# Attention and a gated MLP on one core: two heads per step, loads of 1 KB runs that Pool reshapes two pairs ahead, remainder rows of both heads at the same partitions

## The chip, the cores and the metric

The kernel runs on one NeuronCore of a Trainium2 chip. Time is in device microseconds (us). TensorE (PE) does the matrix products, VectorE (DVE) and ScalarE (ACT) the elementwise work, GpSimd (POOL) the work between SBUF tiles, and SyncE (SP) issues nearly all DMAs from one queue in program order. Each engine works through its own list in order and waits on semaphores for the others.

## The reference

With 8 batches, 8 heads, 576 rows and 64 columns per head:

```python
scores = scale * np.matmul(q, k.transpose(0, 1, 3, 2))          # scale 1/8
thresh = np.max(scores, axis=-1, keepdims=True) - tau           # tau 0.02
attn = exp(where(scores >= thresh, scores, -1e9) - max); attn /= sum(attn) + 1e-9
x = matmul(attn, v), heads side by side: (8, 576, 512)
h = np.maximum(x @ w_in, 0.0); u, v = h[..., :512], h[..., 512:]
v_n = (v - mean(v)) / np.sqrt(var(v) + 1e-06)
v_s = np.einsum('ts,bsd->btd', w_spatial, v_n) + b_spatial[None, :, None]
out = (u * v_s) @ w_out
```

## The kernel before, in words

Two heads of one batch make a **pair**; there are 32 pairs and each has a **slot** of five **steps**, c = 0 to 4. Slot s works on pair s. 576 rows are four chunks of 128 and a remainder of 64 per head. Steps 0 to 3 take one chunk of 128 query rows of both heads; step 4 takes the 64 remainder rows of both heads, head 0 on partitions 0 to 63 and head 1 on 64 to 127.

In one step PE writes the scores of both heads into a PSUM tile `s` (two buffers): the two heads' 512 main columns with K = 64 rows each (lines 368 and 370, side by side in the array) and the 64 remainder columns of both heads through a block-diagonal tile `kd` (line 372). DVE takes the negated row maximum (`negm`, line 386), ACT the exponential (`e`, line 389), and DVE then zeroes what lies below exp(-tau) of the maximum (`p`, line 402; below called the **mask**). The mask of step c is emitted in step c + 1. SP transposes `p` by DMA (`pT`), and a slot later PE multiplies it with `v` (line 218). Step 4 does the same with a block-diagonal `qd` (lines 375, 377), lines 393, 396 and 409, and one transposed tile `pTr`.

Each step also carries **fillers** for PE: in steps 0 to 2 the transposes of the next pair's q, k and remainder (lines 176 and 191), in steps 3 and 4 the product with v of the pair before (line 218, `pv`), and from slot 5 on one piece of the MLP of a finished batch. The MLP of a batch takes four slots: `moe_v` (line 248), `moe_u` (282), `moe_s` (313) and `moe_o` (343), five pieces each, piece c in step c. Slots 5, 9, 13 ... are v slots, 6, 10 ... u slots, 7, 11 ... s slots, 8, 12 ... o slots. A filler's products go into a PSUM tile `f` (two buffers); its evacuation is emitted at the start of the next step, ahead of that step's `negm` and `e`. So in the v slots ACT takes `vrel` (line 253) behind the exponentials of the step before, DVE takes bn_stats and bn_aggr of it (`st`, `mv`, lines 255 and 257) ahead of `negm`, and POOL makes the scale and the normalised `vn` (lines 259 to 266).

The order is written out by hand: engines run the instructions as the Python emits them. q, k and v of pair s + 2 are loaded after step 3 of slot s, into two buffers (`load`, lines 97 to 124, eight DMAs on SP, q and k in runs of 256 bytes); POOL copies v to bf16 (lines 121 to 124) and the remainder blocks into `qd` and `kd` (lines 201 and 203). All of `w_spatial` and the bias is shaped on POOL ahead of the first slot (lines 143 to 161). The normalised attention output `xn` goes through a DMA transpose into `xT` (line 232), on which the v slot's first product waits.

## Time and profile before

| What | us |
|---|---|
| median of 3 runs | 706.11 (704.8 to 706.26) |
| the profiled execution: time / span | 706.51 / 704.7 |
| busy: PE, DVE, ACT, POOL | 517.9, 479.0, 299.2, 209.1 |
| mean granted PE clock | 0.912 of full speed |

The profile lists each instruction with its start and duration in us from the start of the span. A row of the waits says which engine and line waited for what: total us, times, longest. In the timeline a bracket at the end of a row is the idle time of that engine ahead of the instruction and what ended it. PE's busy time counts pipelined matmuls, so it is not PE at its peak.

### The profile page before, as it was taken

The numbers are of one execution on the slowest core, as the hardware profiler recorded it, in microseconds if no ns is written. First come the engines' busy times: TensorE is split into PE (matmuls) and PEld (weight loads), VectorE is DVE, ScalarE is ACT, GpSimd is POOL, SyncE is SP. The second block draws the span as 40 slices with busy tenths as digits, with TensorE's granted clock in tenths as the row PEclk, the third lists the DMA queues.
The fourth block names the chain that finished last, engine by engine and source line by source line (L and its number), as shares of the span: only waits on it lengthen the run. The fifth ranks groups of instructions, "written<-read, shape, count | busy, mean of one in ns | idle before, by whom it ended". The sixth has DMA issues, their size and how long they took to land.

```text
span 704.7 us, 10528 instructions
## 1 busy us (share of the span) xinstructions
PE 517.9 (73%) x3712; PEld 265.5 (38%) x3712; DVE 479.0 (68%) x570; ACT 299.2 (42%) x506; POOL 209.1 (30%) x497
## 2 busy tenths in 40 slices
PE   2177775888856788578858888567896888588876
PEld 1034442444423444244424444234442444244432
DVE  0067776788837787487857888377864888578931
ACT  1044444364524544354443645245352554336332
POOL 5601112451214311344114511143112452145031
PEclk9977777899979999899988999899997999889999
DMA  6947877377956567468693779565575677838531
GB/s 169 145 101 134 147 134 155 54 141 141 179 125 115 114 121 172 102 121 139 127 197 62 144 139 182 122 110 116 107 176 112 113 141 140 195 64 139 97 103 67
DMA packets 297786, 90.94 MB, mean 129 GB/s; under 512 B 283718, under 2 KB 292422, under 8 KB 297606
## 3 DMA queue, kind: packets, MB, share of 16 engines
q1 hardware_dynamic: 296678, 88.71, 64.8%
q0 software_dynamic: 1056, 1.57, 1.4%
q8 instruction: 29, 0.48, 0.3%
q14 instruction: 23, 0.19, 0.1%
HBM read 33.31 MB, written 9.44 MB: 61 GB/s over the span
## 4 chain that ended last, share of the span: by engine, by line
PE 28%; DVE 22%; DMA 14%; SPq 11%; ACT 11%; issue 8%; POOL 5%; POOLq 0%; ACTq 0%; DVEq 0%
DVE negm L386 12%; PE s L368 10%; DMA qn<-in_q_dram 9%; ACT e L389 7%; DVE p L402 6%; SPq L104 5%; PE s L372 4%; DMA xT<-xn 3%; PE f L218 3%; PE f L176 3%; PE f L343 2%; PE f L282 2%; POOL vn L266 2%; SPq L406 2%; SPq L107 2%
## 5 line engine op out<-in xcount | busy, mean ns | idle before, releaser
L389 ACT ACTIVATE e<-s,negm 128x576 f32<-128x576 f32 x256 | 175.7, 738 | 284.0 <-DVE negm L386 284.0
L386 DVE TENSOR_REDUCE negm<-s 128x2 f32<-128x1152 f32 x128 | 172.8, 1350 | 114.2 <-PE s L372 113.6
L402 DVE SCALAR_TENSOR_TENSOR p<-e,ctau 128x1152 bf16<-128x1152 f32 x128 | 181.5, 1418 | 0.0
L368 PE MATMUL s<-kT,qT 64*128 64x512 f32 x256 | 163.3, 721 | 4.2 <-ACT e L389 3.8
L370 PE MATMUL s<-kT,qT 64*128 64x512 f32 x256 | 163.3, 721 | 0.0
L121 POOL CAST v<-vl 128x512 bf16<-128x512 f32 x32 | 19.8, 618 | 291.3 <-DMA vl<-in_v_dram 245.0
L372 PEld LDWEIGHTS s<-kd,qT 128*128 128x128 f32 x256 | 41.4, 203 | 133.2 <-issue 107.7
L372 PE MATMUL s<-kd,qT 128*128 128x128 f32 x256 | 67.4, 348 | 21.6 <-POOL kd L203 21.6
L248 PE MATMUL f<-w_in,xT 128*128 128x512 bf16 x160 | 48.8, 427 | 41.5 <-DMA xT<-xn 41.2
L255 DVE BATCH_NORM_STATS2 st<-vrel 128x6 f32<-128x512 f32 x40 | 27.7, 692 | 73.7 <-ACT vrel L253 73.5
L218 PE MATMUL f<-v,pT 128*128 128x65 bf16 x1280 | 51.1, 193 | 34.1 <-ACT vrel L253 12.9
L176 PE MATMUL f<-identf,qn 128*128 128x128 f32 x128 | 23.8, 317 | 59.0 <-DMA qn<-in_q_dram 52.0
L218 PEld LDWEIGHTS <-pT 128*128 128x128 bf16 x1280 | 49.6, 99 | 40.4 <-issue 34.3
L368 PEld LDWEIGHTS s<-kT,qT 64*128 64x128 f32 x256 | 42.9, 209 | 53.2 <-issue 36.9
L266 POOL TENSOR_SCALAR vn<-vrel,rs,nm 128x512 bf16<-128x512 f32 (+1 forms) x40 | 53.2, 1329 | 4.0
L253 ACT ACTIVATE vrel<-f 128x512 f32<-128x512 f32 x40 | 24.1, 602 | 46.4 <-PE f L248 43.3
L343 PE MATMUL f<-w_o,gT 128*128 128x512 bf16 (+1 forms) x160 | 41.4, 387 | 2.8 <-DVE xn L227 1.7
L370 PEld LDWEIGHTS s<-kT,qT 64*128 64x128 f32 x256 | 42.9, 209 | 0.0
L313 PE MATMUL f<-wsT,vn 128*128 128x512 bf16 x160 | 41.0, 390 | 2.3 <-POOL vn L266 1.4
L396 ACT ACTIVATE e<-s,negm 128x576 f32<-128x576 f32 x32 | 23.7, 741 | 40.6 <-DVE negm L393 40.6
L176 PEld LDWEIGHTS f<-identf,qn 128*128 128x128 f32 x128 | 15.9, 159 | 63.8 <-issue 63.8
L248 PEld LDWEIGHTS <-xT 128*128 128x128 bf16 x160 | 15.8, 108 | 59.1 <-DMA xT<-xn 45.5
(71 smaller groups left out, 633.0 us busy)
## 6 DMA issues: line engine op xcount, KB each, us to landing
qn<-in_q_dram SPq DMA_DIRECT2D x64, 128.0 KB, 2.9
kn<-in_k_dram SPq DMA_DIRECT2D x64, 128.0 KB, 2.8
vl<-in_v_dram SPq DMA_DIRECT2D x32, 256.0 KB, 3.0
out_dram<-o SPq DMA_DIRECT2D x32, 256.0 KB, 2.6
pT<-p SPq DMA_TRANSPOSE x128, 3.3
wsl<-in_moe_w_spatial_dram SPq DMA_DIRECT2D x1, 1152.0 KB, 6.1
qn<-in_q_dram SPq DMA_DIRECT2D x32, 32.0 KB, 2.5
kn<-in_k_dram SPq DMA_DIRECT2D x32, 32.0 KB, 2.4
```

The source lines that it names most:

```text
L176: nc.tensor.transpose(out=t[:, c * P:(c + 1) * P], in_=src[:, c, :], identity=identf)
L218: nc.tensor.matmul(out=t[:, c * 65:c * 65 + 65], lhsT=pts[i, c][:, blk, :], rhs=vt[:, h, vb, :], start=(ki == 0), stop=(ki == 4))
L248: nc.tensor.matmul(out=t, lhsT=xts[b][:, f, c * P:(c + 1) * P], rhs=w_in[:, f, 512:1024], start=(f == 0), stop=(f == 3))
L266: nc.gpsimd.tensor_scalar(out=vn_ring[b % 2][:n, c, :], in0=vrel[:n], scalar1=rs[:n], scalar2=nm[:n], op0=ALU.mult, op1=ALU.add)
L313: nc.tensor.matmul(out=t, lhsT=vn[:, c, f * P:(f + 1) * P], rhs=wsT[:, c, 0:512], start=(c == 0), stop=(c == 4))
L343: nc.tensor.matmul(out=t[:n], lhsT=gs[b][:, f, c * P:c * P + n], rhs=w_o[:, f, :], start=(f == 0), stop=(f == 3))
L368: nc.tensor.matmul(out=s[:, 0:512], lhsT=qT[A, cs], rhs=kT[A, :], start=True, stop=True)
L370: nc.tensor.matmul(out=s[:, 1024:1536], lhsT=qT[Bh, cs], rhs=kT[Bh, :], start=True, stop=True)
L372: nc.tensor.matmul(out=view(s, 512, [[448, 2], [1, 64]]), lhsT=qT[:, cs], rhs=kd_ring[i % 2], start=True, stop=True)
L386: nc.vector.tensor_reduce(out=nm, in_=both, axis=AX.X, op=ALU.max, negate=True)
L389: nc.scalar.activation(out=e[:, h, :], in_=both[:, h, :], func=ACT.Exp, bias=nm[:, h:h + 1])
L402: nc.vector.scalar_tensor_tensor(out=pt, in0=pe.rearrange("p h s -> p (h s)"), scalar=ctau, in1=pe.rearrange("p h s -> p (h s)"), op0=ALU. ...
```

## The change

- **Loads.** Pairs are loaded two at a time (four heads) in odd slots at step 0 for slots s + 3 and s + 4: q and k in two DMAs each, v in five, in runs of 1 KB, into one of two static sets `ql`, `kl`, `vl`. POOL reorders q (and scales it) and k of pair s + 2 at step 1 of slot s (`shape_qk`) and casts v of pair s at step 0 (`shape_v`).
- **Remainder rows.** q and k of a pair now lie in one tile `qkT` of 576 columns, with both remainders in columns 512 to 575. Step 4 is four products of 64 x 64 by 288 columns (two heads, two halves); head 0 writes partitions 0 to 63 of `s`, head 1 partitions 64 to 127 of the same columns. `qd` is gone. `kd`'s product now comes ahead of the other two. The masked remainder is transposed by two DMAs, one per head, into columns 0 to 63 and 64 to 127 of `ptr`, so that both heads' remainders lie at the same partitions; the copy at line 235 is gone.
- **w_spatial** is shaped on POOL in five parts in steps 6 to 10 counted from the start, and the bias in step 12.
- **Steps.** There are two fillers, sorted so that those that ACT evacuates come first. The first, if ACT evacuates it, is evacuated ahead of the step's exponentials, else by DVE behind `negm`; the second, if DVE evacuates it, at the end of its own step, else at the start of the next. The MLP runs 27 steps behind (25 before).
- **Normalisation.** For batches 0 to 6 ACT sums `vrel` as it writes it, POOL makes the negated mean `nmean`, and ACT takes a Square with that bias and a sum in the place of bn_stats and bn_aggr; POOL makes the scale and `vn`. The last batch keeps bn_stats and has `vn`, the u evacuations and every second output copy on DVE.

Where rows move. The order of POOL's instructions at the start, before (`wsb` is the shaped `w_spatial`, the `br` rows are the bias; the block tiles come last):

```order
L143 CAST wsb<-wsl 64x512
L146 CAST wsb<-wsl 64x64
L155 CAST bhi<-brow 1x576
L156 TENSOR_TENSOR br_210<-brow,bhi 1x576
L157 CAST bmid<-br_210 1x576
L158 TENSOR_TENSOR br_211<-br_210,bmid 1x576
L159 CAST blo<-br_211 1x576
L201 TENSOR_SCALAR qd_118<-rem 64x64
L203 COPY kd_116<-rem 64x64
```

and now, from the last fill on:

```order
L94 MEMSET vn_112 64x512
L146 TENSOR_SCALAR qn<-ql_113 128x640
L149 COPY kn<-kl_114 128x640
L229 COPY kd_127<-qkT 64x64
L230 COPY kd_127<-qkT 64x64
L146 TENSOR_SCALAR qn<-ql_113 128x640
L149 COPY kn<-kl_114 128x640
L155 CAST v_107<-vl_115 128x10x64
L146 TENSOR_SCALAR qn<-ql_116 128x640
```

The block tile `kd` of pair 0, on which the first step's scores wait, stood behind all of `wsb` and the bias and now stands behind pair 0's q and k alone; the fills of the new tiles come ahead of it.

SP's queue around the first v slot, before (`qn` to `vl` are the loads of pair 6; the row of `xT` is batch 0's last):

```order
L406 DMA_TRANSPOSE pT<-p_105 128x9x128
L104 DMA qn<-in_q_dram 128x4x64 x2
L107 DMA qn<-in_q_dram 64x2x64
L104 DMA kn<-in_k_dram 128x4x64 x2
L107 DMA kn<-in_k_dram 64x2x64
L112 DMA vl<-in_v_dram 128x2x256
L115 DMA vl<-in_v_dram 64x2x64
L117 DMA vl<-in_v_dram 64x64
L406 DMA_TRANSPOSE pT<-p_106 128x9x128
L232 DMA_TRANSPOSE xT<-xn 128x5x128
L412 DMA_TRANSPOSE pTr<-pr_108 128x5x128
```

and now:

```order
L260 DMA_TRANSPOSE xT<-xn 128x5x128
L437 DMA_TRANSPOSE pT<-p_103 128x9x128
L111 DMA ql_113<-in_q_dram 128x4x256
L114 DMA ql_113<-in_q_dram 64x4x64
L111 DMA kl_114<-in_k_dram 128x4x256
L114 DMA kl_114<-in_k_dram 64x4x64
L122 DMA vl_115<-in_v_dram 128x2x256
L123 DMA vl_115<-in_v_dram 64x2x64
L125 DMA vl_115<-in_v_dram 64x2x256
L127 DMA vl_115<-in_v_dram 64x2x256
L129 DMA vl_115<-in_v_dram 64x2x64
L443 DMA_TRANSPOSE ptr_144<-pr_105 128x5x64
```

The transpose into `xT` moves from behind a group of loads to ahead of one; a group now serves two pairs.

POOL in the steps of `moe_v`, before and now (`rs` is the scale, `nm` its product with the mean):

```order
L259 TENSOR_SCALAR rs<-mv 128x1
L261 TENSOR_TENSOR rs<-rs,mhalf 128x1
L263 TENSOR_SCALAR nm<-mv,rs 128x1
L266 TENSOR_SCALAR vn_114<-vrel,rs,nm 128x512
L121 CAST v_113<-vl 128x2x4x64
```

```order
L311 TENSOR_SCALAR vn_111<-vrel,rs,nm 128x512
L155 CAST v_109<-vl_118 128x10x64
L146 TENSOR_SCALAR qn<-ql_113 128x640
L149 COPY kn<-kl_114 128x640
L299 TENSOR_SCALAR nmean<-sm 128x1
L307 TENSOR_SCALAR rs<-ss 128x1
L309 TENSOR_TENSOR rs<-rs,mhalf 128x1
L310 TENSOR_TENSOR nm<-nmean,rs 128x1
```

ACT's Square of a piece waits for `nmean`, which now stands behind the `vn` of the pieces ahead and behind three instructions of 640 columns.

The diff, cut to its core:

```diff
+    ld_ring = [[const.tile([P, 4, 5, D], F32, name=f"{n}{i}") for n in ("ql", "kl", "vl")]
+               for i in range(2)]
...
+    def load_qk(i, n):
+
+        b, hp = divmod(i, HP)
+        for t, src in zip(ld_ring[i // 2 % 2], (q, k)):
+            t = t[:, 2 * (i % 2):2 * (i % 2) + 2 * n]
+            src = src[b, 2 * hp:2 * hp + 2 * n]
+            nc.sync.dma_start(
+                out=t[:, :, 0:4, :],
+                in_=src[:, 0:512, :].rearrange("h (p c) d -> p h (c d)", c=4))
+            nc.sync.dma_start(out=t[0:64, :, 4, :],
+                              in_=src[:, 512:576, :].rearrange("h p d -> p h d"))
+
+    def load_v(i):
+        b, hp = divmod(i, HP)
+        vv = ld_ring[i // 2 % 2][2].rearrange("p (j h) c d -> p j (h c) d", h=2)
+        va = v[b, 2 * hp:2 * hp + 4].rearrange("(j h) s d -> h j s d", h=2)
+        fold = "j (p c) d -> p j (c d)"
+        nc.sync.dma_start(out=vv[:, :, 0:4, :], in_=va[0, :, 0:512, :].rearrange(fold, c=4))
+        nc.sync.dma_start(out=vv[0:64, :, 4, :],
+                          in_=va[0, :, 512:576, :].rearrange("j p d -> p j d"))
+        nc.sync.dma_start(out=vv[64:128, :, 5:9, :],
+                          in_=va[1, :, 0:256, :].rearrange(fold, c=4))
+        nc.sync.dma_start(out=vv[0:64, :, 6:10, :],
+                          in_=va[1, :, 256:512, :].rearrange(fold, c=4))
+        nc.sync.dma_start(out=vv[64:128, :, 9, :],
+                          in_=va[1, :, 512:576, :].rearrange("j p d -> p j d"))
...
+    def shape_qk(i):
...
+        for w, nm in enumerate(("qn", "kn")):
+            t = qkn.tile([P, 5, 2, D], F32, name=nm)
+            src = ld_ring[i // 2 % 2][w][:, 2 * j:2 * j + 2].rearrange("p h c d -> p c h d")
+            if w == 0:
+                nc.gpsimd.tensor_scalar(out=t, in0=src, scalar1=scale, scalar2=0.0,
+                                        op0=ALU.mult, op1=ALU.add)
+            else:
+                nc.gpsimd.tensor_copy(out=t, in_=src)
...
+    def shape_v(i):
+        j = i % 2
+        nc.gpsimd.tensor_copy(
+            out=v_ring[i % 4][:, :, 0:D],
+            in_=ld_ring[i // 2 % 2][2][:, 2 * j:2 * j + 2].rearrange("p h c d -> p (h c) d"))
...
+        nc.gpsimd.dma_start(
+            out=brow[0:1, 0:512].rearrange("o (c p) -> o c p", c=4),
...
-        for c in range(5):
-            n = P if c < 4 else 64
-            nc.gpsimd.tensor_copy(
-                out=wsb[:n, c, 0:512].rearrange("p (sc sp) -> p sc sp", sc=4),
-                in_=wsl[:n, c, 0:512].rearrange("p (sp sc) -> p sc sp", sc=4))
-            nc.gpsimd.tensor_copy(out=wsb[:n, c, 512:576], in_=wsl[:n, c, 512:576])
-        for c in range(5):
-            nc.sync.dma_start_transpose(out=wsT[:, :, c * P:(c + 1) * P], in_=wsb[:, c, :])
...
+    def shape_ws(c):
...
+        nc.sync.dma_start_transpose(out=wsT[:, :, c * P:(c + 1) * P], in_=wsb[:, c, :])
...
-            nc.scalar.activation(out=dst, in_=hold["t"], func=ACT.Copy,
...
+            nc.scalar.copy(out=qks[i][:, which, 0:512], in_=hold["t"])
...
-                nc.gpsimd.tensor_scalar(out=qd_ring[i % 2][hs, hs], in0=rem[hs, 0:64],
-                                        scalar1=scale, scalar2=0.0, op0=ALU.mult, op1=ALU.add)
-                nc.gpsimd.tensor_copy(out=kd_ring[i % 2][hs, hs], in_=rem[hs, 64:128])
...
+        def ev():
+            nc.scalar.copy(
+                out=qks[i][:, :, 512:576],
+                in_=hold["t"][:, 0:256].rearrange("p (w s) -> p w s", w=2)[:, :, 0:64])
+            kd = kd_ring[i % 2]
+            nc.gpsimd.tensor_copy(out=kd[0:64, 0:64], in_=qks[i][0:64, 1, 512:576])
+            nc.gpsimd.tensor_copy(out=kd[64:128, 64:128], in_=qks[i][64:128, 1, 0:64])
...
-                nc.gpsimd.tensor_copy(out=xts[b][64:128, hp, 512:576],
-                                      in_=xts[b][64:128, hp, 576:640])
...
-            nc.vector.bn_stats(out=st, in_=vrel)
-            mv = small.tile([P, 2], F32, name="mv")
-            nc.vector.bn_aggr(out=mv, in_=st)
...
+            if b == B - 1:
+                nc.scalar.activation(out=vrel, in_=hold["t"], func=ACT.Relu)
...
+                nc.vector.tensor_scalar(out=rs, in0=mv[:, 1:2], scalar1=1e-6, scalar2=1.0,
+                                        op0=ALU.add, op1=ALU.mult)
+                nc.gpsimd.tensor_tensor(out=rs, in0=rs, in1=mhalf, op=ALU.pow)
+                nc.vector.tensor_scalar(out=dst, in0=vrel[:n], scalar1=mv[:n, 0:1],
+                                        scalar2=rs[:n], op0=ALU.subtract, op1=ALU.mult)
...
+            nc.scalar.activation(out=vrel, in_=hold["t"], func=ACT.Relu, accum_out=sm)
+            nmean = small.tile([P, 1], F32, name="nmean")
+            nc.gpsimd.tensor_scalar(out=nmean, in0=sm, scalar1=-1.0 / 512, scalar2=0.0,
                                     op0=ALU.mult, op1=ALU.add)
...
+            def rest():
+                sq = vr.tile([P, 512], BF16, name="sq")
+                ss = small.tile([P, 1], F32, name="ss")
+                nc.scalar.activation(out=sq, in_=vrel, func=ACT.Square, bias=nmean,
+                                     accum_out=ss)
+                nc.gpsimd.tensor_scalar(out=rs, in0=ss, scalar1=1.0 / 512, scalar2=1e-6,
+                                        op0=ALU.mult, op1=ALU.add)
+                nc.gpsimd.tensor_tensor(out=rs, in0=rs, in1=mhalf, op=ALU.pow)
+                nc.gpsimd.tensor_tensor(out=nm, in0=nmean, in1=rs, op=ALU.mult)
+                nc.gpsimd.tensor_scalar(out=dst, in0=vrel[:n], scalar1=rs[:n], scalar2=nm[:n],
+                                        op0=ALU.mult, op1=ALU.add)
+            later.append(rest)
...
+            if f < 4 and b == B - 1:
+                nc.vector.tensor_scalar(out=us[b][:, f, 0:512], in0=t, scalar1=0.0, scalar2=0.0,
+                                        op0=ALU.max, op1=ALU.add)
...
+            if b == B - 1 and c % 2:
+                nc.vector.tensor_copy(out=o[:n], in_=hold["t"][:n])
...
+            return nc.tensor.matmul(out=out, lhsT=qk[hs, 0, m], rhs=qk[hs, 1, lo:lo + n],
+                                    start=True, stop=True)
+        if c < 4:
+            nc.tensor.matmul(out=view(s, 512, [[448, 2], [1, 64]]),
+                             lhsT=qk[:, 0, c * P:(c + 1) * P], rhs=kd_ring[i % 2],
+                             start=True, stop=True)
+            mm(0, s[:, 0:512], 0, 512)
+            mm(1, s[:, 1024:1536], 64, 512)
...
+        for lo, off in ((0, 224), (288, 512)):
+            for h in range(2):
+                mm(h, s[64 * h:64 * h + 64, off:off + 288], lo, 288)
...
+            dst = ptr_ring[i % 3]
+            nc.sync.dma_start_transpose(out=dst[:, :, 0:64], in_=pt[0:64, 64:704])
+            nc.sync.dma_start_transpose(out=dst[:, :, 64:128], in_=pt[64:128, 0:640])
...
+            s = scores(i, c)
+        while held:
+            held.pop(0)()
+        if f1:
+            f1[1]()
+            if f1[0] == "act":
+                f1[2]()
+        if i is not None:
+            nh = 2 if c < 4 else 1
+            nm = small.tile([P, 2], F32, name="negm")
+            nc.vector.tensor_reduce(out=nm[:, 0:nh], in_=s, axis=AX.X, op=ALU.max, negate=True)
+        if f1 and f1[0] == "dve":
+            f1[2]()
+        done = list(later)
+        later.clear()
...
+        if unmasked:
+            mask()
...
+        for f in done:
+            f()
+        if f2:
+            f2[1]()
+            if f2[0] == "dve":
+                f2[2]()
             else:
...
-        for mm, ev in fillers:
-            mm()
-            pend_ev.append(ev)
...
+                held.append(f2[2])
...
+    LAG = 27
...
+        load_qk(0, 1)
+        shape_qk(0)
+        for f in (qk_main(0, 0), qk_main(0, 1), qk_rem(0)):
+            f[1]()
+            f[2]()
+        load_qk(1, 1)
+        shape_qk(1)
+        load_v(0)
+        load_qk(2, 2)
+        load_v(2)
...
+            if i is not None:
+                if c == 1 and slot + 2 < NPAIR:
+                    shape_qk(slot + 2)
+                if c == 0:
+                    shape_v(slot)
+                if c == 0 and slot % 2 and slot + 3 < NPAIR:
+                    load_qk(slot + 3, 2)
+                    load_v(slot + 3)
+                if g == 3:
+                    load_weights()
+                if 6 <= g <= 10:
+                    shape_ws(g - 6)
+                if g == 12:
+                    shape_bias()
+            fs = []
+            if slot + 1 < NPAIR and c < 3:
+                fs.append(qk_rem(slot + 1) if c == 2 else qk_main(slot + 1, c))
+            if 1 <= slot <= NPAIR and c >= 3:
+                fs.append(pv(slot - 1, c - 3))
+            if g >= LAG:
+                fs.append(moe_job(g - LAG))
+            fs.sort(key=lambda f: f[0])
+            step(i, c, fs[0] if fs else None, fs[1] if len(fs) > 1 else None)
+        while held:
+            held.pop(0)()
```

280 lines of the change are left out of this document (107 added, 173 removed).

## The prediction

> **What bounds the kernel now.** I read the busy times first, then the waits, then the timeline of DVE from one row maximum to the next, because each step has exactly one and they mark its pace.
>
> ```profile
> PE 517.9 (73%) x3712; PEld 265.5 (38%) x3712; DVE 479.0 (68%) x570; ACT 299.2 (42%) x506; POOL 209.1 (30%) x497
> DVE negm L386 <- PE s L372: 113.6, 65, 32.3
> DVE st L255 <- ACT vrel L253: 73.5, 24, 7.9
> PE f L176 <- DMA qn<-in_q_dram: 52.0, 28, 5.0
> PE s L372 <- POOL kd L203: 21.6, 1, 21.6
> ```
>
> No engine is full: PE, the busiest, is busy 517.9 of a span of 704.7. The waits form loops, and where they lie differs by slot. These are the starts of slot 0, of slot 2 with the two row maxima after it, and of slots 5, 17, 18, 19 and 31:
>
> ```profile
> 33.19 1.36 DVE L386 TENSOR_REDUCE negm<-s 128x2 f32<-128x1152 f32 x1 [32.29 <-PE s L372]
> 64.56 1.35 DVE L386 TENSOR_REDUCE negm<-s 128x2 f32<-128x1152 f32 x1
> 70.41 1.36 DVE L386 TENSOR_REDUCE negm<-s 128x2 f32<-128x1152 f32 x1 [3.78 <-PE s L372]
> 73.01 1.35 DVE L386 TENSOR_REDUCE negm<-s 128x2 f32<-128x1152 f32 x1
> 115.48 1.35 DVE L386 TENSOR_REDUCE negm<-s 128x2 f32<-128x1152 f32 x1
> 361.75 1.36 DVE L386 TENSOR_REDUCE negm<-s 128x2 f32<-128x1152 f32 x1 [0.86 <-PE s L372]
> 390.45 1.32 DVE L386 TENSOR_REDUCE negm<-s 128x2 f32<-128x1152 f32 x1
> 406.11 1.36 DVE L386 TENSOR_REDUCE negm<-s 128x2 f32<-128x1152 f32 x1 [0.36 <-PE s L372]
> 652.51 1.36 DVE L386 TENSOR_REDUCE negm<-s 128x2 f32<-128x1152 f32 x1 [0.31 <-PE s L372]
> ```
>
> The span divides into 33.2 before the first step, 82.3 for slots 0 to 4 (115.48 - 33.19), 537.0 for slots 5 to 30 (652.51 - 115.48), and 52.2 from there to the end. A v slot took 28.7 (361.75 to 390.45), the u slot behind it 15.7 (to 406.11). Seven of the 26 slots in the middle are v slots, and they take 7 x 28.7 = 201 of the 537.
>
> In slot 2 the first step takes 5.85 (64.56 to 70.41) and the next 2.60. The 3.25 between them is the wait of PE's transposes for the q that SP has only just loaded. A v slot has two stalls:
>
> ```profile
> 277.60 1.28 SPq L104 DMA_DIRECT2D qn<-in_q_dram  x2
> 286.14 1.21 SPq L232 DMA_TRANSPOSE xT<-xn  x1
> 288.81 0.61 PE L248 MATMUL f<-w_in,xT 128*128 128x512 bf16 x1 [6.27 <-DMA xT<-xn]
> 298.34 1.37 ACT L389 ACTIVATE e<-s,negm 128x576 f32<-128x576 f32 x2 [2.35 <-DVE negm L386]
> 299.75 0.62 ACT L253 ACTIVATE vrel<-f 128x512 f32<-128x512 f32 x1
> 300.40 0.70 DVE L255 BATCH_NORM_STATS2 st<-vrel 128x6 f32<-128x512 f32 x1 [0.83 <-ACT vrel L253]
> 301.29 1.32 DVE L386 TENSOR_REDUCE negm<-s 128x2 f32<-128x1152 f32 x1
> ```
>
> First, SP issues a whole group of loads from 277.60 before the transpose into `xT` at 286.14, and PE stands 6.27 for it. Second, each of the following steps is a closed loop: exponentials 1.37, then `vrel` .62 behind them, then `st` .70, then the row maximum that the next exponentials need. ACT and DVE take turns.
>
> **The change part by part.** *Start.* The first row maximum, at 33.19, waits 21.6 for `kd`, which stands on POOL behind `wsb` and the bias. Those move to steps 6 to 12. What is left on POOL ahead of it: the fills (.15 to .5 each; they end at 5.2 before, and I put the larger set's end at 7.5), then q and k reshaped. For a reshaping of 640 columns the nearest row is
>
> ```profile
> L121 POOL CAST v<-vl 128x512 bf16<-128x512 f32 x32 | 19.8, 618 | 291.3 <-DMA vl<-in_v_dram 245.0 <-PE f L176 26.9 <-PE f L313 11.0
> L261 POOL TENSOR_TENSOR rs<-rs,mhalf 128x1 f32<-128x1 f32 x40 | 22.1, 554 | 3.3
> L143 POOL CAST wsb<-wsl 128x512 bf16<-128x512 f32 x4 | 4.3, 1070 | 0.9 <-DMA wsl<-in_moe_w_spatial_dram 0.9
> ```
>
> 618 ns x 640/512 = .77. A cast that collects single elements took 1.07 for 512, so 1.34 for 640 is the dear end; the new ones move runs of 64 elements, as L121 does, and write 4 bytes, so I take .9. Then 7.5 + .9 + .9 = 9.3, transposes of k 1.1 at the low clock, two copies .9, two `kd` copies .5 (64 columns each, so below L121's .62), cold scores 2.8: first row maximum near 14.5, **-18.7**. Later fills or dearer copies would cost up to 3.
>
> *Slots 0 to 4.* q and k are now loaded two to three slots ahead and reshaped at step 1 for use two slots on, so the 3.25 goes: 16.9 - 3.25 = 13.65 a slot, where DVE alone sets the pace. The shaping of `w_spatial` (4 x 1.07 + 1.06 and five small ones), the bias and the weights' DMA issues now lie on POOL inside these slots. I add 4 for a backlog that reaches `kd`. 5 x 13.65 + 4 = 72.3 against 82.3: **-10**, bounds -14 and 0.
>
> *Slots 5 to 30, other than v.* Here PE's own work is the floor:
>
> ```profile
> L375 PE MATMUL s<-kT,qd 128*128 128x512 f32 x64 | 33.2, 600 | 2.1 <-ACT e L389 2.1
> 73.29 0.69 PE L368 MATMUL s<-kT,qT 64*128 64x512 f32 x1
> 74.67 0.51 PE L218 MATMUL f<-v,pT 128*128 128x65 bf16 x11
> 390.41 0.63 PE L176 MATMUL f<-identf,qn 128*128 128x128 f32 x4 [1.03 <-DMA qn<-in_q_dram]
> 393.78 0.66 PE L176 MATMUL f<-identf,kn 128*128 128x128 f32 x4 [0.40 <-ACT qT L180]
> 394.27 1.03 PE L282 MATMUL f<-xT,w_in 128*128 128x512 bf16 x4
> 395.23 0.69 PE L368 MATMUL s<-kT,qT 64*128 64x512 f32 x1
> 399.85 0.80 PE L218 MATMUL f<-v,pT 128*128 128x65 bf16 x20
> ```
>
> From start to start, a chunk's scores take 1.38 (73.29 to 74.67), a set of transposes .49, an MLP piece .96, a product with v .80 (399.85). A slot is 4 x 1.38 + 2 x .49 + 5 x .96 + 2 x .80 + remainder scores 1.1 (two of .60 in line 375, that overlap) and transposes .3 = 14.3. The best whole slot, the u slot from 390.45, took 15.66 and holds the 1.03 wait for q, which goes. I take **15.1** for u and o slots (.8 of hand-overs left). In s slots DVE is the longer: two of its steps stand 3.20 apart (334.68 to 337.88), .60 over the 2.60, so 13.65 + 5 x .6 = **16.65**; nothing of that is touched.
>
> ```profile
> 334.68 1.35 DVE L386 TENSOR_REDUCE negm<-s 128x2 f32<-128x1152 f32 x1
> 337.88 1.36 DVE L386 TENSOR_REDUCE negm<-s 128x2 f32<-128x1152 f32 x1
> 298.38 1.83 POOL L266 TENSOR_SCALAR vn<-vrel,rs,nm 128x512 bf16<-128x512 f32 x1
> 151.21 0.77 POOL L266 TENSOR_SCALAR vn<-vrel,rs,nm 128x512 bf16<-128x512 f32 x1
> 151.39 1.79 DVE L402 SCALAR_TENSOR_TENSOR p<-e,ctau 128x1152 bf16<-128x1152 f32 x1
> 302.54 1.41 DVE L402 SCALAR_TENSOR_TENSOR p<-e,ctau 128x1152 bf16<-128x1152 f32 x1
> ```
>
> *SP and the small moves.* A slot's issues change by one more transpose (1.21, as at 286.14; the remainder takes two) and 3.5 fewer loads (.64 each, from 277.60), so SP loses about 1 a slot. The loads that `xT` passes land 1.2 later, and nobody wants them for two slots. The block tile's product now comes first in a step, at the same length. `qd` and the copy at line 235 leave POOL some .7 a slot, which I count against the queue's gaps. Evacuating a filler ahead of the exponentials, or on DVE behind `negm`, lets `f` come free in the same step; while PE sets the pace its evacuation (.6 to .7) has a step of 2.6 to 3.2 to hide in, so **0**; were it on the path in all 65 steps of the u and o slots, 65 x .6 = 39 and a time of 615, which the range holds.
>
> *v slots.* Three things go: the `xT` wait (its transpose now stands ahead of the loads, and the MLP runs two steps later), the q wait, and bn_stats, for which ACT does a Square (.6 like `vrel`) in its idle 58%. What is new is a chain over POOL: `vrel`'s sum, `nmean`, Square, scale, `vn`. ACT's Square stands in the next step behind that step's exponentials and waits for `nmean`; behind a late Square stand the next evacuation and exponentials, hence DVE. So the question is whether POOL keeps up. A piece costs it the power .55 (line 261), `vn` .77 (151.21) and three smaller instructions on one column, which with gaps I put at .9: 2.2, for five 11.0; reshaping costs .9 + .9 + .77 + .5 = 3.1 a slot: 14.1 in all. The rows above show POOL standing still under a mask: `vn` took .77 clear of one (151.21) and 1.83 beside one (298.38). The masks hold 4 x 1.41 + .81 = 6.45 of a slot, so POOL has 15.1 - 6.45 = 8.65 of it and is 5.5 short. Part is carried into the slots behind, as the next MLP stage needs `vn` only ten steps after a piece; I charge 4.7, a v slot of **19.8**, nearer to the full debt because `nmean` queues behind everything. Bounds 0 and 5.5, and above that if masks yield to POOL.
>
> They can: the mask at 151.39 took 1.79, not 1.41, when a `vn` had started .18 before it. The Trainium skill ("SBUF — State Buffer", section "SBUF: two separate sides") says that a DVE instruction with two SBUF inputs and a POOL instruction that reads SBUF exclude one another for a whole instruction, and that whichever starts first goes first. By that rule, with which these rows agree, moving work to POOL can lengthen DVE's masks; rival (b) below prices this from the rows alone.
>
> The middle: 7 x 19.8 + 7 x 15.1 + 6 x 16.65 + 6 x 15.1 = 434.8 against 537.0: **-102.2**.
>
> *End.* The last batch's `vn` chain moves to a DVE that has no steps left to serve, so its length should not change much; two more s pieces, .96 each, fall behind the last slot, where part of them lies under PE's wait for the last `xT`: **+1**, bounds -3 and +3.
>
> *Sum.* -18.7 - 10 - 102.2 + 1 = -129.9, span 704.7 - 129.9 = 574.8. The profiled execution took 706.51, 1.8 over its span and .4 over the runs' median of 706.11. So **576 us**.
>
> **The rivals.** (a) *POOL's shortage is hidden.* `nm`, scale and 128x1 instructions run between masks and the debt is carried forward: v slots at 15.1, 7 x 4.7 less, **543**. For it: POOL is busy 30% now. Against: the queue's order, `nmean` behind three reshapings.
>
> (b) *POOL is dearer than that.* .3 on each of some 130 masks (39) and 3 more on each v slot (21): **636**. For it 151.39; against, most masks start when POOL is already waiting.
>
> (c) *The remainder scores get slower.* Four products of 64 x 64 by 288 columns, two at a time to different partitions of the same columns, take the place of two. If the two heads' run one after the other, PE gains .8 a slot, which it has least to spare: +26, **602**. No row of before has two row groups write the same columns. The Trainium skill ("TensorEngine Tiling (Array Packing)", Gotcha 1: PSUM Pressure) says that different row tiles cannot access one PSUM bank at the same time, which is this case.
>
> (d) *The loads don't hide.* DMA engines are already crowded in places:
>
> ```profile
> q1 hardware_dynamic: 296678, 88.71, 64.8%
> 343.00:366.00 23.00, 17.22 (x121) 8.57 (x119) 17.03 (x20) 12.01 (x21) 4.16 (x9) 0.98 0.91 179
> ```
>
> 64.8% of 704.7 is 457 us a DMA engine; in 576 that is 79%, and over 343 to 366 the share (next to last number) was .91. A group of nine loads in a burst would hold up the mask transposes by some 4, sixteen times: **640**. Longer runs speak against it.
>
> (e) *Slower.* POOL sets the pace of every slot. Per batch it has 23.4 of work (4 x 3.1 + 11.0) beside 25.8 under masks, 49 of 63. To make slots of 20, at which the gain at start and middle is used up, it has to cost 2.3 times that; at 2.6 times, 21.7 a slot x 32 + 54 = **747**. The nearest row for it, L143, shows only 1.07/.62 = 1.7.
>
> **How the numbers follow.** Forecast (556 to 596) .52, (a) .17, (b) .13, (c) .07, (d) .06, (e) .04, a change that comes to nothing .01. Differences under .2%, 1.4 us, can't be told from none. Faster .94, same .01, slower .05. The range, two in ten left out, runs from 536 to 636: below (a)'s 543 with a shorter start, up to (b).
>
> **What would show it.** First row maximum at 13 to 17; v steps under 4 and no `st` wait; no wait for q or `xT` above a few us in all; u and o slots at 15 to 15.5; ACT's Square waiting for POOL's `nmean` some 30 us in all (near 0: (a)); mean mask under 1.5 (1.7: (b)); remainder scores under 1.1 a slot (1.8: (c)). It is wrong if the waits for `kd` or `nmean` stand in every slot, or PE waits for the reshaped q.

## The result and the profile after

The changed kernel takes 628.44 us (621.81 to 630.72), the kernel before in the same comparison 705.45: a ratio of .890 with a 95% interval of .883 to .898. That is faster, by 77 us where 129.9 were forecast. The profiled execution has a span of 625.7, so 79.0 less than the 704.7 before; the parts below are parts of these two spans.

The first row of its busy times, the waits that the account below rests on, and DVE's row maxima at the starts of slots 0, 1, 2, 5, 10, 11 and 31 (`negm` is at line 460 now):

```profile
PE 502.8 (80%) x3790; PEld 264.4 (42%) x3840; DVE 471.1 (75%) x516; ACT 327.9 (52%) x605; POOL 223.1 (36%) x398
DVE negm L460 <- PE s L415: 60.0, 68, 13.5
PE f L245 <- DMA ptr<-pr: 59.0, 16, 7.3
POOL wsb L176 <- DMA wsl<-in_moe_w_spatial_dram: 14.2, 1, 14.2
DVE p L434 <- DMA pT<-p: 11.7, 3, 7.9
ACT sq L305 <- POOL nmean L299: 10.4, 10, 3.6
...
14.44 1.36 DVE L460 TENSOR_REDUCE negm<-s 128x2 f32<-128x1152 f32 x1 [13.55 <-PE s L415]
27.76 1.34 DVE L460 TENSOR_REDUCE negm<-s 128x2 f32<-128x1152 f32 x1
59.98 1.34 DVE L460 TENSOR_REDUCE negm<-s 128x2 f32<-128x1152 f32 x1
108.44 1.35 DVE L460 TENSOR_REDUCE negm<-s 128x2 f32<-128x1152 f32 x1
197.03 1.36 DVE L460 TENSOR_REDUCE negm<-s 128x2 f32<-128x1152 f32 x1 [0.84 <-PE s L415]
213.17 1.36 DVE L460 TENSOR_REDUCE negm<-s 128x2 f32<-128x1152 f32 x1
567.36 1.35 DVE L460 TENSOR_REDUCE negm<-s 128x2 f32<-128x1152 f32 x1
```

The waits for `qn`, `xT` and `st`, 52.0, 41.2 and 73.5 us before, are gone from the list, but for 3.7 of `st`. A wait of PE for `ptr`, the transposed remainder rows, has taken their place. The span divides like this:

| part | before | forecast | after |
|---|---|---|---|
| to the first row maximum | 33.2 | 14.5 | 14.4 |
| slots 0 to 4 | 82.3 | 72.3 | 94.0 |
| slots 5 to 30 | 537.0 | 434.8 | 458.9 |
| slot 31 to the end | 52.2 | 53.2 | 58.3 |

The start came out to .1 us. Slots 0 to 4 got longer, mainly because slot 1 takes 32.2 (27.76 to 59.98). In slots 5 to 30 the slots differ by whether they are even or odd: slot 10 takes 16.1, slot 11 takes 19.5. This is slot 11, SP's queue with two row maxima, the product that waits and the scores behind it:

```profile
215.42 0.54 SPq L111 DMA_DIRECT2D ql<-in_q_dram  x1
...
220.61 0.61 SPq L129 DMA_DIRECT2D vl<-in_v_dram  x1
221.31 1.22 SPq L443 DMA_TRANSPOSE ptr<-pr  x1
222.30 1.34 DVE L460 TENSOR_REDUCE negm<-s 128x2 f32<-128x1152 f32 x1
222.58 1.24 SPq L444 DMA_TRANSPOSE ptr<-pr  x1
225.19 0.32 PE L245 MATMUL f<-v,ptr 128*128 128x65 bf16 x5 [2.87 <-DMA ptr<-pr]
226.55 2.19 PE L415 MATMUL s<-qkT 64*64 64x288 f32 x8
228.78 0.76 DVE L460 TENSOR_REDUCE negm<-s 128x1 f32<-128x576 f32 x1 [0.59 <-PE s L415]
```

The nine loads of a group occupy SP from 215.42 to 221.2. Behind them stand the two transposes of slot 10's remainder, which land only at 225.2, and the product with v in step 3 needs them. Step 3 takes 6.48 (222.30 to 228.78). Over the twelve odd slots from 5 to 27, all of which carry a group, step 3 takes 91.3 in all; in a slot without that wait it takes 3.22 or 3.81 by the MLP stage (read from the kernel with single loads, below), 42.2 for the twelve. So 49 us lie there, and up to 12 more in the same step of slots 1 and 3.

The even slots 6, 10 ... 26 hold the last two v pieces of a batch and take 16.1 each. Slot 30 is the one slot of that kind with no group of loads in the slot ahead, and it takes 19.3, of which step 1 is 7.31 (550.80 to 558.11):

```profile
550.77 0.19 POOL L299 TENSOR_SCALAR nmean<-sm 128x1 f32<-128x1 f32 x1
550.80 1.36 DVE L460 TENSOR_REDUCE negm<-s 128x2 f32<-128x1152 f32 x1 [0.65 <-PE s L415]
550.99 0.72 ACT L305 ACTIVATE sq<-vrel,nmean 128x512 bf16<-128x512 f32 x1 [3.58 <-POOL nmean L299]
558.11 1.36 DVE L460 TENSOR_REDUCE negm<-s 128x2 f32<-128x1152 f32 x1 [3.05 <-PE s L415]
```

There ACT's Square stands 3.58 for POOL's `nmean`, in the whole kernel 10.4. This is the wait that the prediction charged to every v slot.

### The profile page after: what moved, and what is told of

It is laid out like the page before. It is cut to its first block, busy times and chain, and to the rows that moved or that the text cites. A ratio compares the mean times of both kernels' runs of the same rounds, so it can differ in the third digit from the quotient of the medians.

```text
span 625.7 us, 10432 instructions
## 1 busy us (share of the span) xinstructions
PE 502.8 (80%) x3790; PEld 264.4 (42%) x3840; DVE 471.1 (75%) x516; ACT 327.9 (52%) x605; POOL 223.1 (36%) x398
## 4 chain that ended last, share of the span: by engine, by line
PE 36%; DVE 23%; DMA 15%; issue 8%; POOL 7%; ACT 6%; SPq 4%; POOLq 0%; ACTq 0%; DVEq 0%
PE s L415 14%; DVE p L434 10%; DVE negm L460 9%; DMA ptr<-pr 8%; PE f L245 6%; PE f L358 5%; DMA kl<-in_k_dram 3%; DMA wsl<-in_moe_w_spatial_dram 3%; PE f L324 2%; PE f L275 2%; ACT e L468 2%; ACT sq L305 2%; PE s L418 2%; PE f L388 2%; PE f L208 2%
## 5 line engine op out<-in xcount | busy, mean ns | idle before, releaser
L460 DVE TENSOR_REDUCE negm<-s 128x2 f32<-128x1152 f32 (+1 forms) x160 | 197.3, 1233 | 60.8 <-PE s L415 60.0
L434 DVE SCALAR_TENSOR_TENSOR p<-e,ctau 128x1152 bf16<-128x1152 f32 x128 | 189.2, 1478 | 13.2 <-DMA pT<-p 11.7
L415 PE MATMUL s<-qkT 64*128 64x512 f32 (+1 forms) x768 | 198.1, 611 | 1.2 <-ACT e L468 1.0
L415 PEld LDWEIGHTS s<-qkT 64*128 64x128 f32 (+1 forms) x768 | 58.2, 181 | 35.1 <-issue 12.5
L212 ACT COPY qkT<-f 128x512 f32<-128x512 f32 x64 | 37.5, 586 | 63.8 <-PE f L208 63.8
L245 PE MATMUL f<-v,ptr 128*128 128x65 bf16 x320 | 22.7, 207 | 59.0 <-DMA ptr<-pr 59.0
L245 PE MATMUL f<-v,pT 128*128 128x65 bf16 x1280 | 56.2, 201 | 15.0 <-DMA pT<-p 10.4
L418 PE MATMUL s<-kd,qkT 128*128 128x128 f32 x256 | 55.8, 301 | 9.2 <-ACT e L468 6.9
L418 PEld LDWEIGHTS s<-kd,qkT 128*128 128x128 f32 x256 | 45.3, 197 | 25.0 <-ACT e L468 8.3
L146 POOL TENSOR_SCALAR qn<-ql 128x640 f32<-128x640 f32 x32 | 47.7, 1489 | 3.0 <-DMA ql<-in_q_dram 2.8
L324 PE MATMUL f<-xT,w_in 128*128 128x512 bf16 x121 | 34.1, 396 | 13.0 <-ACT vrel L297 5.6
L245 PEld LDWEIGHTS <-ptr 128*128 128x128 bf16 x320 | 16.1, 105 | 60.6 <-DMA ptr<-pr 56.0
L297 ACT ACTIVATE vrel<-f 128x512 f32<-128x512 f32 x35 | 20.8, 595 | 29.7 <-PE f L275 29.3
L396 ACT COPY o<-f 128x512 f32<-128x512 f32 (+1 forms) x38 | 22.2, 583 | 24.1 <-PE f L388 22.3
L255 DVE TENSOR_TENSOR xn<-f,r 128x320 bf16<-128x320 f32 x64 | 31.5, 491 | 2.2
```

The costliest lines, as they stand in the source:

```text
L146: nc.gpsimd.tensor_scalar(out=t, in0=src, scalar1=scale, scalar2=0.0, op0=ALU.mult, op1=ALU.add)
L212: nc.scalar.copy(out=qks[i][:, which, 0:512], in_=hold["t"])
L245: nc.tensor.matmul(out=t[:, c * 65:c * 65 + 65], lhsT=pts[i, c][:, blk, lo:lo + P], rhs=vt[:, 5 * h + j, :], start=(j == 0), stop=(j == 4))
L324: nc.tensor.matmul(out=t, lhsT=w_in[:, m, f * P:(f + 1) * P], rhs=xts[b][:, m, 0:512], start=(m == 0), stop=(m == 3))
L415: return nc.tensor.matmul(out=out, lhsT=qk[hs, 0, m], rhs=qk[hs, 1, lo:lo + n], start=True, stop=True)
L418: nc.tensor.matmul(out=view(s, 512, [[448, 2], [1, 64]]), lhsT=qk[:, 0, c * P:(c + 1) * P], rhs=kd_ring[i % 2], start=True, stop=True)
```

## Experiments

All are edits of the changed kernel, and their times are compared with its 628.44 us. Ratios are to the kernel before. Code is cut to the lines that matter.

### The group of loads behind the remainder's transposes

```diff
-                if c == 0 and slot % 2 and slot + 3 < NPAIR:
+                if c == 1 and slot % 2 and slot + 3 < NPAIR:
                     load_qk(slot + 3, 2)
                     load_v(slot + 3)
```

> The changed kernel with one edit: the group of nine loads is issued at step 1 of the odd slots, behind the two transposes of the previous pair's remainder, and not at step 0 ahead of them. The burst itself stays. Theory (queue order: the remainder's transposes stand behind 5.9 us of load issues on SP, and PE's product with v waits for them): the wait of PE for ptr falls from 59.0 us to under 8, step 3 of the odd slots from 6.5 to 9.0 down to 3.2 to 3.8, 13 x 4.6 = 60 less, 568 us. Rival (occupancy: 1.77 MB in one burst fill the DMA engines, and whatever transposes come next are late): step 3 or the step behind it stays long, 610 to 628 us.

613.78 us, ratio .872 (.867 to .877). The waits:

```profile
DVE p L434 <- DMA pT<-p: 52.0, 16, 6.4
...
PE f L245 <- DMA ptr<-pr: 4.1, 3, 1.8
```

The wait for `ptr` went from 59.0 to 4.1, as the theory of the queue's order said, but 52.0 came back at another place: the masks now wait until one of the three `p` tiles is transposed, because the chunks' transposes stand behind the burst instead (in slot 11 SP issues the nine loads from 214.34 to 220.15 and the transposes of `p` from 220.26 on). The long step moved from 3 to 4 (slot 11: 3.81 and 5.22, 6.48 and 3.93 before). Where the burst stands decides mostly who waits for it. The theory was right about the wait for `ptr` and wrong about the time, which came out as the rival had it. The rival's reason, full DMA engines, has the smaller share in the changed kernel's wait: in slot 11 the loads hold up the issue of the two transposes by 5.9 (215.42 to 221.31), while from issue to landing they take 2.5 to 4.9 behind the groups of slots 5 to 27, and 2.3 to 2.5 in most slots without a group.

### One load to a step

```diff
...
-                    load_qk(slot + 3, 2)
-                    load_v(slot + 3)
+                    todo.extend(load_qk(slot + 3, 2) + load_v(slot + 3))
+                if todo:
+                    todo.pop(0)()
```

(`load_qk` and `load_v` return their DMAs in place of issuing them. The condition is step 1 of the odd slots.)

> The changed kernel with the nine loads of a group taken apart: one load in each of nine steps, from step 1 of the odd slot on. Queue order: as with the group at step 1, 568 us give or take 6, since a single load ahead of a transpose costs only .6. Occupancy: clearly better than the group at step 1, by 30 us or more.

584.17 us, ratio .832 (.829 to .835): 44 less than the changed kernel, 30 less than the burst one step later. The same bytes in the same number of DMAs, so what cost the time was nine of them in a row.

```profile
ACT sq L316 <- POOL nmean L310: 38.0, 18, 4.1
POOL kn L160 <- DMA kl<-in_k_dram: 33.9, 8, 6.1
POOL qn L157 <- DMA ql<-in_q_dram: 19.5, 4, 8.1
DVE p L445 <- DMA pT<-p: 15.3, 7, 6.3
...
PE f L256 <- DMA ptr<-pr: 7.9, 4, 3.4
```

The time stayed 16 us above the 568 expected, and a wait has grown: ACT's Square for POOL's `nmean`, 38.0 (10.4 in the changed kernel). The slots with the last two v pieces (6, 10, 14 ... 26) take 17.0 to 20.2, where they took 16.1 while the load stall stood ahead of them. This is the shortage of POOL that was forecast. Here the loads of k and q come too late for POOL as well (33.9 and 19.5).

### w_spatial shaped later, and the weights loaded in pieces

First the shaping alone:

```diff
-                if 6 <= g <= 10:
-                    shape_ws(g - 6)
-                if g == 12:
+                if 16 <= g <= 20:
+                    shape_ws(g - 16)
+                if g == 22:
                     shape_bias()
```

> The changed kernel with w_spatial shaped in steps 16 to 20 and the bias in step 22 (6 to 10 and 12 before); the weights' DMAs stay in step 3. Theory (slot 1 takes 32.2 us because the 2.7 MB of weights delay the transposes of p, and DVE and PE wait for these): slot 1 stays within 2 us, time within 4 of 628. Rival (POOL's 14.2 us wait for w_spatial blocks its queue, and the steps stand behind it): slot 1 falls by 12 to 18, 612 us.

625.34 us, ratio .888 (.885 to .891), not to be told from the changed kernel, and slot 1 at 30.2. POOL's wait of 14.2 for `w_spatial` was not what held slot 1. These rows of the changed kernel show what did: the issue of one transpose of `p` behind the weights' DMAs takes 9.82 (in slot 11 it takes 1.3), and DVE and PE stand for the transposes:

```profile
33.88 9.82 SPq L437 DMA_TRANSPOSE pT<-p  x1
39.02 1.42 DVE L434 SCALAR_TENSOR_TENSOR p<-e,ctau 128x1152 bf16<-128x1152 f32 x1 [7.92 <-DMA pT<-p]
44.78 0.46 PE L245 MATMUL f<-v,pT 128*128 128x65 bf16 x5 [5.38 <-DMA pT<-p]
```

The four transposes of `p` issued between 20 and 34 us land 13.6 after their issue in the median; over the whole kernel the median is 3.3. So here it is mainly the transfers that are late, where in slot 11 it was mainly SP's queue.

Then the DMAs in pieces (`w_in` in steps 12, 14, 16 and 18, `w_spatial` in 13, 15 ... 21, `w_out` in 24, 26, 28 and 30, the bias shaped in step 29):

```diff
-                if g == 3:
-                    load_weights()
-                if 6 <= g <= 10:
-                    shape_ws(g - 6)
+                load_weights(g)
+                if 19 <= g <= 27 and g % 2:
+                    shape_ws((g - 19) // 2)
...
```

> The changed kernel with the weights' DMAs in pieces: w_spatial in five parts in steps 13 to 21, shaped three steps after the part's load, w_in in four parts in steps 12 to 18, w_out in four in steps 24 to 30. Theory (the weights' DMAs in one go delay the transposes of p): slot 1 falls from 32.2 to 17 to 20 (its load group stays), slots 2 to 5 gain at most 3 in all, 613 us. Rival (POOL's wait for w_spatial): the same here, so the run with only the shaping later tells the two apart; if neither moves slot 1, it is the load group of slot 1 alone.

621.41 us, ratio .880 (.875 to .885), where 613 were expected: little gained, if anything. Slot 1 fell to 20.8, and what is left over a plain slot's 13.65 is the load group's stall (step 3 takes 10.2). But slots 3, 5 and 6 grew (19.6 to 23.6, 18.6 to 22.2, 16.2 to 18.7), so that slots 0 to 6 took 126.9 in all against 128.7. So the weights' DMAs made 11.4 of slot 1's length, and in pieces among the bursts of loads they cost nearly as much in other slots.

### Square or bn_stats

```diff
-            nc.scalar.activation(out=vrel, in_=hold["t"], func=ACT.Relu, accum_out=sm)
+            nc.scalar.activation(out=vrel, in_=hold["t"], func=ACT.Relu)
+            nc.vector.bn_stats(out=st, in_=vrel)
+            nc.vector.bn_aggr(out=mv, in_=st)
...
```

> The changed kernel with bn_stats and bn_aggr on DVE in place of ACT's sums and Square, for batches 0 to 6; the new order of evacuations and all else stay. Theory (the Square takes .87 us a piece off a DVE that is nearly full in the steps of v): 35 x .6 to .87 = 20 to 30 us slower than 628, 650 us. Rival (the gain in the slots of v came from the earlier evacuation and the earlier transposes alone, and POOL's nmean in ACT's queue costs what the Square saves): within 5 of 628, or up to 10 faster.

644.36 us, ratio .916 (.909 to .922): 16 slower. The exchange is worth that much, less than the 20 to 30 expected: slots 10, 14, 18 ... went from 16.1 to 17.5 and step 2 of the slots ahead of them from 2.6 to 5.1. Those two make 23 for six batches; step 4 of the slots ahead, behind the load stall, gave back 8.0 (24.5 to 16.5 in sum).

### POOL's reshaping of q and k done twice

```diff
+            nc.gpsimd.tensor_copy(out=t, in_=src)
             if w == 0:
                 nc.gpsimd.tensor_scalar(out=t, in0=src, ...
```

> The changed kernel with POOL writing each reshaped q and k twice (a plain copy of 640 columns first, .7 us each, 1.4 us more a slot). The prediction's step (POOL is short in the slots of v and ACT's Square waits for nmean): the slots of v grow by the 1.4 and more, with masks beside POOL longer: 25 to 40 slower, 660 us. Rival (POOL's shortage is hidden, the debt is carried over): within 8 of 628.

651.11 us, ratio .924 (.920 to .929): 23 slower for 1.4 us more of POOL's time a slot. Slots 10, 14, 18 and 22 rise from 16.1 to between 19.9 and 20.8, 22 in all six with slots 6 and 26; the other slots add 2.2 in sum and the start 1.3. In slot 18:

```profile
356.72 1.83 POOL L145 COPY kn<-kl 128x640 f32<-128x640 f32 x1
357.97 1.36 DVE L461 TENSOR_REDUCE negm<-s 128x2 f32<-128x1152 f32 x1
358.62 0.72 POOL L150 COPY kn<-kl 128x640 f32<-128x640 f32 x1
359.30 1.40 POOL L300 TENSOR_SCALAR nmean<-sm 128x1 f32<-128x1 f32 x1
360.73 0.72 ACT L306 ACTIVATE sq<-vrel,nmean 128x512 bf16<-128x512 f32 x1 [3.02 <-POOL nmean L300]
...
366.52 1.36 DVE L461 TENSOR_REDUCE negm<-s 128x2 f32<-128x1152 f32 x1 [5.87 <-PE s L416]
```

`nmean` stands behind the reshapings, ACT stands for it, and one step lasts 8.55 (357.97 to 366.52). POOL's slack in these slots is below what the copies added.

### The last batch as before

vn on POOL, u on ACT again for the last batch:

```diff
-            if f < 4 and b == B - 1:
+            if False:
                 nc.vector.tensor_scalar(out=us[b][:, f, 0:512], in0=t, ...
...
```

> The changed kernel with the last batch's vn on POOL and its u evacuations on ACT, as in the kernel before (its second output copies stay on DVE). Theory (behind the last xT, 32.5 us now against 26.4 before, because DVE does five chains of 2.2 us and only then the u evacuations, for which PE waits 5.5): 5 to 6 us less, 622 us. Rival (the tail is longer for the two more s pieces): within 1.5 of 628 in the tail.

618.21 us, ratio .880 (.875 to .885). From slot 31 to the end it takes 52.2 against 58.3. The rest of the difference, 7.1 in the profiled executions, lies ahead of slot 31, 5.0 of it in steps 3 and 4 of the odd slots from 5 on, which this edit does not touch. The rows of the changed kernel that show the 6:

```profile
605.40 1.27 DVE L339 TENSOR_SCALAR uT<-f 128x512 bf16<-128x512 f32 x2
606.13 3.57 PE L324 MATMUL f<-xT,w_in 128*128 128x512 bf16 x8 [5.50 <-DVE uT L339]
```

DVE works through five chains of normalisation, each with a wait for POOL's power, before it takes the first u; PE has no free `f` and stands 5.50.

### What is left when the burst is gone

Single loads a slot earlier (q and k in the even slot, v in the odd one) and the weights in pieces:

```diff
-                if c == 1 and slot % 2 and slot + 3 < NPAIR:
-                    todo.extend(load_qk(slot + 3, 2) + load_v(slot + 3))
+                if c == 1 and slot % 2 == 0 and slot + 4 < NPAIR:
+                    todo.extend(load_qk(slot + 4, 2) + load_v(slot + 4))
...
```

> The changed kernel with each load in a step of its own, the four of q and k in the even slot ahead (so POOL's reshaping finds them landed) and the five of v in the odd slot, and with the weights in pieces: w_in in steps 6 to 18, w_spatial in steps 20 to 28 and shaped three steps later, w_out in steps 30 to 36. Theory (queue order, and POOL's chain held up by loads that come late, are what is left to gain): against 584.2 with the loads one to a step, the waits of POOL for kl and ql (53 us) vanish and with them the 4.4 to 8.2 us steps in the slots of v, 15 to 20 less, and slot 1 falls from 25 to 15 or 16, 10 less: 555 us, every slot from 7 to 29 between 14.2 and 16.5. Rival (the DMA engines' total work sets the pace once the bursts are gone): 575 to 585, with waits for pT and ptr spread over all slots.

587.12 us, ratio .835 (.830 to .839): no gain on 584, and slot 1 took 21.1 where 15 or 16 were expected. POOL's waits for loads vanished (33.9 and 19.5 to 1.9 and .5), yet Square's wait for `nmean` was 44.1 and slots 10, 14, 18, 22 and 26 stayed at 18.0 to 20.2. So the late loads weren't the cause; POOL's own order was tried next. Shaping `w_spatial` in steps 23 to 31 put more on POOL where the first v pieces run, and slot 6 rose to 26.9. Then POOL's reshaping was moved behind the v pieces of those slots:

```diff
-                if c == 1 and slot + 2 < NPAIR:
+                late = slot % 4 == 2 and slot > 2
+                if c == (3 if late else 1) and slot + 2 < NPAIR:
                     shape_qk(slot + 2)
-                if c == 0:
+                if c == (3 if late else 0):
                     shape_v(slot)
```

> The kernel with single loads ahead and weights in pieces (587.1 us), and one edit more: in every fourth slot (6, 10, 14 ...), where the last two v pieces run, POOL reshapes q, k and v at step 3, behind the pieces, and not at steps 0 and 1 between them. Theory (ACT's Square waits for nmean behind the three reshapings; this shortage of POOL is what the load stall had hidden in the changed kernel): slots 10, 14, 18, 22 and 26 fall from 18.0 to 20.2 to about 16.2, ACT's wait for nmean from 44 to under 20, 12 less, 575 us. Rival (POOL's total work, not its order, is too much there): slots within 1 us, time within 4 of 587.

579.4 us, ratio .822 (.818 to .826): 8 less. The five slots took 16.2, 17.1, 18.6, 18.5 and 17.1. The wait for `nmean` fell only from 44.1 to 37.7. The order was part of it. That the rest is the length of POOL's chain itself, piece after piece, was not tested; for it speaks slot 30 of the changed kernel, which has the wait although POOL reshapes no q and k in it (there is no pair 32). The same edit on the changed kernel with its burst:

> The changed kernel with that one edit alone (reshaping at step 3 of slots 6, 10, 14 ...), the burst of nine loads left at step 0 of the odd slots. Theory (while PE stands for the remainder's transposes in step 3 of slots 5, 9, 13 ..., POOL works off its debt, so its order makes no difference): within 4 of 628, slots 10, 14 ... within .6 of 16.1. Rival (the shortage counts beside the load stall): 10 or more faster.

624.27 us, ratio .888 (.883 to .892), not to be told from the changed kernel, and those slots at 16.13 as without it. While PE stands for `ptr` in step 3 of the odd slot, POOL catches up, so its order costs nothing there; in slot 30, with no such stall ahead, its shortage shows. The two losses do not add: one hides the other.

All parts together (the last two edits, the last batch as before, `w_spatial` loaded in steps 7 to 19 and shaped in 13 to 25, `w_in` in steps 11 and 18, `w_out` in 33 and 38) come in two versions. In the first the bias is shaped ahead of the last part of `w_spatial`, whose transpose overwrites it, so that the last 64 rows come out without their bias:

> All of it together: single loads ahead, reshaping behind the v pieces, the last batch's vn on POOL and u on ACT, and the weights in pieces earlier (w_spatial in steps 7 to 19 and shaped in 13 to 25, w_in in two parts in steps 11 and 18, w_out in two in steps 33 and 38). Against 587: 12 less in slots 10 to 26, 6 less behind the last slot, slots 5 and 6 from 45 to about 33: 557 us. Rival (the DMA engines are full in slots 1 to 5, so earlier weights only move the wait there): 568 us.

568.6 us, which is what the rival had. The tail is 6 shorter, as expected, but slots 10, 14, 18, 22 and 26 gained 5 for the 12 and slots 2 and 3, where weights' pieces now stand, grew by 11. In the second version the bias stands behind:

```diff
-                if g == 23:
+                if g == 26:
                     shape_bias()
```

> All parts together as in the run before, with the bias shaped in step 26, behind the last part of w_spatial, whose transpose overwrote the bias of the last rows when it was shaped in step 23. One step's move of 5.7 us of POOL's work: 569 us give or take 5; against the kernel before a ratio of .81.

566.71 us (564.9 to 569.36), ratio .807 (.802 to .812), 62 below the changed kernel and the best of all. Its first row, and the largest of its waits that are left on the path:

```profile
PE 484.6 (86%) x3840; PEld 254.2 (45%) x3840; DVE 464.7 (82%) x502; ACT 327.4 (58%) x609; POOL 240.5 (43%) x415
DVE negm L484 <- PE s L439: 45.9, 49, 13.5
ACT sq L329 <- POOL nmean L323: 26.3, 12, 4.1
```

Slot 1 takes 13.65 there, though slots 2 and 3 with the weights' pieces still take 19.

## Why the prediction was right, and where it was off

The direction and the range held. The forecast gain was 53 us too large, 50.9 in the spans: 21.7 of it lie in slots 0 to 4, 24.1 in slots 5 to 30, 5.1 behind them. In the largest term a stall that was priced at nothing and a shortage that did not show partly made up for each other, so that the time landed within the range is in part luck.

**Start, -18.7.** Right: 14.44 for 14.5, and its parts too: the fills end at 7.3 for 7.5, reshaping q and k takes 1.4 for 1.8, the cold scores 2.8 for 2.8.

**Slots 0 to 4, -10, measured +11.7.** The term looked at POOL's backlog alone. The run with the shaping moved showed that POOL is not the cause. Moving the weights' DMAs (2832 KB) from ahead of the first slot into step 3 puts them before the transposes of `p`, and the run with the weights in pieces takes 11.4 out of slot 1. Of the 18.6 that slot 1 takes over a plain slot's 13.65 the other 7.2 are its load group. The start's gain was partly paid back there.

**"The loads that xT passes land 1.2 later, and nobody wants them for two slots."** This is the step that failed most. It asked who waits for the loads, and not who stands behind them on SP. The remainder's transposes did, and the product with v three steps later waited for them: 59.0 us. Rival (d) had the burst that holds up transposes, at "some 4, sixteen times" and 640, with a chance of .06; measured were 49 in twelve slots, 4.1 each, and up to 12 in two more. But it gave crowded DMA engines as the reason and named the masks' transposes; the rows show SP's queue above all, and the remainder's transposes. The trace of before showed what it takes, loads at .6 each on SP ahead of a transpose that PE waits for (`xT`, 288.81), and the same look at `ptr` would have given it a larger chance.

**v slots at 19.8.** The number came true and its reason did not. The v pieces now lie in steps 2 to 4 of one slot and steps 0 and 1 of the next, and these five steps take 19.75 in the mean of the seven batches. In six of them 4.3 of that is the load stall in step 3, so without it they would take some 15.5, near rival (a)'s 15.1. But not because POOL has room: the seventh, with no stall, took 18.7 with the wait for `nmean`; with POOL's reshaping doubled slots 6, 10 ... 26 grew by 3.7 each; and with the loads one to a step the v steps took 17.9 in the mean. That is 2.8 over the 15.1 where 4.7 were charged. The shortage of POOL is real and was sized too large, and the load stall covered it. The sign "Square waits some 30 us" stands the same way: 10.4 in the changed kernel, 38.0 with the loads taken apart. That the forecast's 576 is within 2% of the 584 of the kernel that differs only in the burst is again a sum in which errors cancel: slots 0 to 4 took 86.8 there for 72.3, slots 5 to 30 422.8 for 434.8, the end 57.9 for 53.2.

**u, s and o slots at 15.1, 16.65 and 15.1.** Counted in the same way, by the five steps that hold a stage's pieces, they take 15.6, 20.9 and 14.5. The s steps hold the second load stall and lost 25.3 in six batches, which is the whole of what slots 5 to 30 missed. In the best kernel the three take 15.4, 16.3 and 14.5, so the terms were right but for the stall.

**End, +1, measured +6.1.** Mis-sized, outside its bounds of -3 and +3: the u evacuations behind the normalisation on DVE were not counted.

**Rival (b)** fell: DVE's masks have a mean of 1478 ns (1418 before), 7.7 us in all for 39. POOL is the one that gives way, as its reshaping shows:

```profile
L434 DVE SCALAR_TENSOR_TENSOR p<-e,ctau 128x1152 bf16<-128x1152 f32 x128 | 189.2, 1478 | 13.2 <-DMA pT<-p 11.7 <-ACT e L468 1.4
L146 POOL TENSOR_SCALAR qn<-ql 128x640 f32<-128x640 f32 x32 | 47.7, 1489 | 3.0 <-DMA ql<-in_q_dram 2.8
L149 POOL COPY kn<-kl 128x640 f32<-128x640 f32 x32 | 22.8, 714 | 6.2 <-DMA kl<-in_k_dram 6.1
7.36 0.73 POOL L146 TENSOR_SCALAR qn<-ql 128x640 f32<-128x640 f32 x1
```

The reshaping of q falls under a mask in most slots and takes 1.49 in the mean, where the first one, clear of any mask, took .73 (7.36); that of k, of the same size right behind it, takes .71. This agrees with the exclusion that the Trainium skill ("SBUF — State Buffer", section "SBUF: two separate sides") states.

**Rival (c)** fell as well. A chunk's scores and the remainder's, of the changed kernel:

```profile
100.30 1.13 PE L415 MATMUL s<-qkT 64*128 64x512 f32 x4
102.48 1.19 PE L415 MATMUL s<-qkT 64*64 64x288 f32 x8
```

The profile lists each of these products twice: two products of 512 columns take 1.13, four of 288 take 1.19, 1024 and 1152 columns at about the same rate. So the two heads' remainders run side by side as the two heads of a chunk do, though they write the same columns of PSUM on different partitions. (Behind a load stall the same four take 2.19, at 226.55 above; the last section says why.) The Trainium skill ("TensorEngine Tiling (Array Packing)", Gotcha 1: PSUM Pressure) says that different row tiles cannot use one bank at the same time; for tiles that write different partitions this measurement shows otherwise.

What stays open: in slots 18 and 22 a step of 5.7 to 8.2 us was left in the four kernels with single loads a slot earlier, with ACT waiting for `nmean`; how much of it is the masks' hold on POOL and how much the chain's length was not separated.

## What to carry to other kernels

When a group of DMAs is moved on a queue, list what stands behind it on that queue and when each of those is needed; here the burst cost its own reader little (9 us of waits) and whoever came next a lot (59), and moving it one place mostly changed who that was. Taking it apart, one transfer to a step, gained 44 us. A stall gives other engines time to catch up, so a shortage that is right by the sum may not show until the stall is removed; price both, and expect the second when the first is mended.

## What was not expected

The clock that TensorE was granted rose as the gaps closed, from a mean of .918 in the changed kernel to .953 with single loads and .975 in the best. In the changed kernel it was .79 over the 8 us around a load stall and 1.00 in steps without one (the third number from the end of each row):

```profile
204.00:212.00 8.00, 7.15 (x78) 4.06 (x77) 6.78 (x8) 5.41 (x10) 6.95 (x12) 1.00 0.63 105
222.00:230.00 8.00, 5.13 (x54) 2.87 (x51) 5.01 (x7) 1.74 (x3) 1.08 (x2) 0.79 0.91 152
```

A stall of PE therefore cost more than its own length: the remainder's scores behind the stall of slot 11 took 2.19 (226.55) where they take 1.19 in a slot without one, and PE's busy time for the same products fell from 502.8 us in the changed kernel to 484.6 in the best.
